# Two ordering dependencies for the w1 groups of a gated attention and MLP kernel

**Chip and metric.** One core of one Trainium2 chip. The metric is the device time of one execution in microseconds (us). The span that the profile shows is about 1.7 us shorter than that time. PE is TensorE, POOL GpSimd, ACT ScalarE, DVE VectorE and SP SyncE. The granted clock is what the trace records of PE's clock, as a share of full speed; 0.5 is called half clock here.

## What is computed

The input x has 2048 tokens of 640 features. Branch A is linear attention with 32 heads of 20; branch B is a two-stage mixer with layernorms; a sigmoid gate mixes them. Cut to what matters here:

```python
a = linear_attention(x, wqkv) @ wo           # needs phi(k), phi(q), and k^T v per head
h = gelu(layernorm(x) @ w1)                  # token shifts by 1 and 2, then
x1 = x + shift(h) @ w2
b = x1 + gelu(layernorm(x1) @ w3) @ w4
out = g * a + (1 - g) * b
```

The kernel never forms v. It builds G = x^T phi(k) (640 x 640), in five tiles of 128 rows ("features" 0 to 4), and from G and the v weights the k^T v of each head ("KV groups").

## The kernel before

The program is a list of items (matmul groups, normalizations, loads) in several streams. At build time a greedy scheduler takes the item that could start first by a rough time model, and this fixes each engine's instruction order. At run time every engine works through its own order and waits on semaphores. An item's dependency is a pair (item, lag): the named item must already have been *issued*, and with a number, the model also waits for its end. With `None` only the order is fixed.

```python
for d, lag in it["deps"]:
    if d not in done:
        ok = False
        break
    if lag is None:
        continue
    v = done[d] + 100.0
    if v > est:
        est = v
...
key = (max(est, t_pe), 0 if it["dur"] == 0.0 else 1, -cp[n])
```

Three groups of items meet in the stretch in question:

```python
# G: features 1..4 in two parts each, over token tiles 0..10 and 11..15
for i in range(1, KD):
    IT.add("GT", ("ga", i), 2.98, lambda i=i: gt_step(i, 0, NT - 5), deps=[(("k", NT - 1), 0.0)] if i == 1 else [])
    IT.add("GT", ("g", i), 1.36, lambda i=i: gt_step(i, NT - 5, NT), deps=[(("g0", NT - 1), 0.0)])

# first layernorm: statistics of a chunk of 4 tiles, then normalize a tile (both on POOL),
# then transpose it by DMA into xnT
for u in range(NT):
    if u % 4 == 0:
        IT.add("S1", ("s1", u // 4), 0.0, lambda u=u: stats1(u // 4), deps=[(("k", u + 3), 1.8)])
    ...
    IT.add("N1", ("n1", u), 0.0, lambda u=u: normalize(1, u, st1), deps=d1)
    IT.add("T1", ("t1", u), 0.0, lambda u=u: t_xn(1, u), deps=[(("n1", u), 1.1)])

# w1: four chunks of 4 token tiles, five groups of 5 matmuls each; j == 0 needs the 4 tiles
for c in range(NCH):
    for j in range(KD):
        deps = [(("t1", u), 0.9) for u in range(4 * c, 4 * c + 4)] if j == 0 else []
        if c == 0 and j == 0:
            deps.append((LAST_EXP, None))
        IT.add("W1", ("w1", c, j), 1.08, lambda c=c, j=j: w1_group(c, j), deps)
```

In the profile, G's matmuls carry line L783 (`ps<-pk_tok,x_tok`), w1's L606 (`ps<-xnT,w_59`), the KV groups' L939 (`ps<-GT,wv`). L831 is dummy matmuls of constants, which the kernel's `warmup` issues at the start.

## Time and profile before

| | before |
|---|---|
| time, median (first three runs) | 270.7 us |
| span of the profiled run | 269.1 us |
| PE busy | 97% of the span |
| mean granted clock | 0.994 |
| PE stall on the transposed x | 2.62 us |

The page's busy line, its clock by 40 slices (tenths of full speed), the shares by engine of the chain that ended last, and the w1 group with its busy time, mean, idle before it and releaser:

```profile
PE 262.0 (97%) x1729; PEld 137.1 (51%) x1729; DVE 146.7 (55%) x242; ACT 107.8 (40%) x218; POOL 92.0 (34%) x148
...
PEclk9999999999799999999999999999999999999999
...
PE 92%; POOL 4%; DMA 1%; ACT 1%; DVE 0%; issue 0%; POOLq 0%
...
L606 PE MATMUL ps<-xnT,w_59 128*128 128x512 bf16 x100 | 25.6, 399 | 2.6 <-DMA xnT<-xn 2.6
```

PE is busy nearly all the time, so a change that leaves its work as it is must remove idle time of PE or give its matmuls a faster clock. The single slice with a 7, and the 2.6 us of idle before w1, are the only blemishes after the start. PE's timeline (start, duration, line, operands, count; idle before it in brackets) places them:

```profile
53.71 12.66 PE L783 MATMUL ps<-pk_tok,x_tok 128*128 128x512 bf16 x92
68.99 5.08 PE L606 MATMUL ps<-xnT,w_59 128*128 128x512 bf16 x15 [2.62 <-DMA xnT<-xn]
73.91 1.52 PE L783 MATMUL ps<-pk_tok,x_tok 128*128 128x512 bf16 x10
75.27 1.24 PE L606 MATMUL ps<-xnT,w_59 128*128 128x512 bf16 x5
76.34 3.15 PE L783 MATMUL ps<-pk_tok,x_tok 128*128 128x512 bf16 x22
```

PE runs out of issued G work at 66.37 us and stands until tile 3 of the normalized x has landed. There was more G work, but it stood behind w1 in PE's order (the next 10 matmuls of G began at 73.91 us). The windows view over these microseconds has PE busy in the first pair of columns and the granted clock third from the end:

```profile
66.00:69.00 3.00, 0.38 (x8) 0.24 (x6) 2.93 (x3) 0.00 (x0) 3.00 (x4) 1.00 0.63 121
...
70.00:71.00 1.00, 1.00 (x5) 0.40 (x3) 1.00 (x1) 0.60 (x1) 1.00 (x2) 0.61 2.69 146
71.00:72.00 1.00, 1.00 (x3) 0.30 (x2) 0.96 (x2) 0.00 (x0) 0.80 (x1) 0.50 0.04 4
72.00:73.00 1.00, 1.00 (x4) 0.42 (x3) 0.47 (x1) 0.60 (x1) 0.00 (x0) 0.50 0.87 182
73.00:74.00 1.00, 1.00 (x5) 0.38 (x4) 0.00 (x0) 0.00 (x0) 0.68 (x1) 0.68 0.77 140
```

So the stall was followed by 3.413 us of half clock (70.22 to 73.64 us in the trace's clock record). Why tile 3 was late is read from POOL's timeline: tile 0 was normalized at 51.03 us, then came the statistics of the last chunk, then seven more tiles in a row. Tile 3 is the third of these.

```profile
51.03 0.87 POOL L628 TENSOR_SCALAR xn<-x_tok,st_54 128x640 bf16<-128x640 bf16 x1
54.76 0.26 POOL L628 TENSOR_SCALAR st_54<-lr 128x4 f32<-128x4 f32 x1 [2.86 <-ACT lr L662]
...
61.78 10.02 POOL L628 TENSOR_SCALAR xn<-x_tok,st_54 128x640 bf16<-128x640 bf16 x7
```

The chain of waits (start, duration, what) shows the three tiles and then the DMA transpose of tile 3, which landed at 68.74 us:

```profile
61.79 4.35 POOL xn L628 x3
66.16 2.58 DMA xnT<-xn
```

### The profile page before, as it was taken

To read this page: it belongs to the slowest core of one execution; us is meant where nothing else is said; L and a number is where in the kernel's file an instruction comes from. 1 tells how busy PE (TensorE), PEld (TensorE's weight loads), DVE (VectorE), ACT (ScalarE), POOL (GpSimd) and SP (SyncE) were. 2 spreads that over 40 slices of the span, in tenths; PEclk is the share of its full clock that TensorE was granted. 3 is DMA by queue.
4 is the path that set the end of the run, shared out by engine and by line. 5 is a ranking of instruction groups with operands and counts; after the bars stand their busy time and mean duration, and the time that the engine had idled before them with its cause. 6 is when DMAs were issued, how large, how long until landed. Compare 5 with 4: busy or idle time off the path is not lost.

```text
span 269.1 us, 4338 instructions
## 1 busy us (share of the span) xinstructions
PE 262.0 (97%) x1729; PEld 137.1 (51%) x1729; DVE 146.7 (55%) x242; ACT 107.8 (40%) x218; POOL 92.0 (34%) x148
## 2 busy tenths in 40 slices
PE   7999999998799999999999999999999999999995
PEld 4555555554255555555444555554555455445553
DVE  1587877899700787999796786512212121122232
ACT  3496777642126459575762202112221412121000
POOL 4013995779762007387850103101120011021020
PEclk9999999999799999999999999999999999999999
DMA  7765979732957971533856831220000200002011
GB/s 217 224 97 146 210 154 128 229 42 49 119 103 139 394 236 26 74 65 58 77 113 126 106 73 24 51 97 0 2 0 0 100 0 0 2 0 100 0 49 49
DMA packets 50355, 24.77 MB, mean 92 GB/s; under 512 B 41756, under 2 KB 48925, under 8 KB 50336
## 3 DMA queue, kind: packets, MB, share of 16 engines
q1 hardware_dynamic: 49184, 21.23, 36.3%
q0 software_dynamic: 1152, 3.28, 5.3%
q8 instruction: 13, 0.21, 0.4%
q14 instruction: 6, 0.05, 0.1%
HBM read 12.04 MB, written 2.62 MB: 55 GB/s over the span
## 4 chain that ended last, share of the span: by engine, by line
PE 92%; POOL 4%; DMA 1%; ACT 1%; DVE 0%; issue 0%; POOLq 0%
PE ps L606 61%; PE ps L1100 21%; PE ps L783 3%; PE ps L853 2%; POOL xn L628 2%; POOL st_54 L636 2%; PE ps L831 1%; PE ps L1082 1%; PE ps L1022 1%; DMA xnT<-xn 1%; PE ps L617 1%; PE ps L939 1%; PE ps L854 1%; DVE x_tok L645 0%; POOL st_54 L628 0%
## 5 line engine op out<-in xcount | busy, mean ns | idle before, releaser
L662 ACT ACTIVATE h2T<-ps 128x512 bf16<-128x512 f32 x52 | 31.0, 596 | 83.8 <-PE ps L606 83.7
L606 PE MATMUL ps<-xnT,w_58 128*128 128x512 bf16 x260 | 60.9, 379 | 0.0
L1100 PE MATMUL ps<-w_84,h2T 128*128 128x512 bf16 (+1 forms) x416 | 58.8, 299 | 0.0
L628 POOL TENSOR_SCALAR abx<-x_tok,stg 128x640 f32<-128x640 bf16 x16 | 13.9, 874 | 107.6 <-DVE x_tok L645 71.2
L1100 PEld LDWEIGHTS ps<-w_84,h2T 128*128 128x128 bf16 x416 | 32.7, 98 | 27.8 <-issue 1.3
L645 DVE SCALAR_TENSOR_TENSOR x_tok<-ps,stg,abx 128x640 bf16<-128x640 f32 (+2 forms) x17 | 14.3, 845 | 51.7 <-PE ps L1100 51.7
L606 PEld LDWEIGHTS ps<-xnT,w_58 128*128 128x128 bf16 x260 | 24.0, 98 | 24.9 <-issue 1.0
L645 DVE SCALAR_TENSOR_TENSOR abx<-ps,stg,abx 128x640 f32<-128x640 f32 x16 | 14.1, 882 | 27.9 <-PE ps L606 24.9
L606 PE MATMUL ps<-xnT,w_59 128*128 128x512 bf16 x100 | 25.6, 399 | 2.6 <-DMA xnT<-xn 2.6
L662 ACT ACTIVATE hsT<-ps 128x512 bf16<-128x512 f32 (+1 forms) x32 | 18.8, 593 | 23.0 <-PE ps L606 22.6
L662 ACT ACTIVATE Er<-ps 128x640 bf16<-128x640 f32 x32 | 22.4, 704 | 13.7 <-PE ps L606 8.5
L661 ACT ACTIVATE junk<-x_tok 128x640 bf16<-128x640 bf16 x32 | 23.6, 736 | 2.0 <-DVE x_tok L643 1.7
L783 PE MATMUL ps<-pk_tok,x_tok 128*128 128x512 bf16 (+1 forms) x160 | 24.2, 299 | 0.0
L606 PE MATMUL ps<-M_sb,pqnT 128*128 128x512 bf16 (+1 forms) x160 | 24.1, 299 | 0.0
L606 PE MATMUL ps<-w_60,hsT 128*128 128x512 bf16 (+1 forms) x160 | 23.7, 299 | 0.0
L643 DVE SCALAR_TENSOR_TENSOR x_tok<-ps,x_tok 128x640 bf16<-128x640 f32 x16 | 13.0, 821 | 19.2 <-PE ps L606 17.6
L606 PE MATMUL ps<-wkg,xT 128*128 128x512 bf16 (+1 forms) x150 | 22.6, 299 | 0.0
L606 PEld LDWEIGHTS ps<-M_sb,pqnT 128*128 128x128 bf16 x160 | 13.1, 98 | 12.2 <-issue 0.6
L628 POOL TENSOR_SCALAR xn<-x_tok,st_54 128x640 bf16<-128x640 bf16 x16 | 17.8, 1123 | 4.3 <-DMA xnT<-xn 4.3
L606 PEld LDWEIGHTS ps<-w_60,hsT 128*128 128x128 bf16 x160 | 13.2, 98 | 12.1 <-DVE Lt L636 0.3
L628 POOL TENSOR_SCALAR xn<-x_tok,st_55 128x640 bf16<-128x640 bf16 x16 | 16.8, 1057 | 4.9 <-DMA xnT<-xn 4.5
L606 PE MATMUL ps<-wq,xT 128*128 128x512 bf16 (+1 forms) x120 | 18.3, 299 | 0.0
(74 smaller groups left out, 265.1 us busy)
## 6 DMA issues: line engine op xcount, KB each, us to landing
w_58<-in_B_w_dram SPq DMA_DIRECT2D x1, 2160.0 KB, 9.6
w_84<-in_B_w_dram SPq DMA_DIRECT2D x1, 2080.0 KB, 12.3
x_tok<-in_A_x_dram SPq DMA_DIRECT2D x3, 640.0 KB, 5.9
out_dram<-x_tok SPq DMA_DIRECT2D x3, 640.0 KB, 3.5
wq<-in_A_wqkv_dram SPq DMA_DIRECT2D x5, 160.0 KB, 4.0
wkg<-in_A_wqkv_dram SPq DMA_DIRECT2D x5, 160.0 KB, 4.2
wv<-in_A_wqkv_dram POOLq DMA_DIRECT2D x1, 800.0 KB, 6.7
wo_aug<-in_A_wo_dram POOLq DMA_DIRECT2D x5, 150.0 KB, 5.1
```

Of the source, the lines that this page charges most:

```text
L606: ins = e.matmul(out_ap, l, r, start=(i == 0), stop=(i == n - 1))
L617: ins = e.transpose(o, s_, ident[:])
L628: return engf(lambda e: e.tensor_scalar(out_ap, in_ap, s1, s2, op0, op1), rd, [out_ap], cost=cost)
L636: return engf(lambda e: e.tensor_tensor(out_ap, a, b_, op), [a, b_], [out_ap], cost=cost)
L643: return dve(lambda e: e.scalar_tensor_tensor(out_ap, in0, scalar, in1, op0, op1, accum_out=accum), rd, [out_ap, accum], cost=cost + 70.0)
L645: return dve(lambda e: e.scalar_tensor_tensor(out_ap, in0, scalar, in1, op0, op1), rd, [out_ap], cost=cost)
L661: return act(lambda e: e.activation(out_ap, in_ap, func, bias=bias, scale=scale, accum_out=accum), rd, wr, cost=cost)
L662: return act(lambda e: e.activation(out_ap, in_ap, func, bias=bias, scale=scale), rd, wr, cost=cost)
L783: ins = e.matmul(o, l, r, start=(t0 + q_ == 0), stop=(t0 + q_ == NT - 1))
L831: ins = e.matmul(ps[:, b, :], ones_c[:, 0:128], ones_c[:, 128:640], start=True, stop=True)
L853: e.matmul(ps[:, b, 0:512], l, w[:, k, 0:512], start=(k == 0), stop=(k == KD - 1))
L1100: ins = e.matmul(o, l, r, start=False, stop=(i == KFF - 1))
```

## The change

The intent is to keep PE on G, which needs nothing late, until xnT is there: w1's first group may be issued only once the first part of G feature 4 has been, and chunk 1's w1 groups only behind all of G.

```diff
             if c == 0 and j == 0:
                 deps.append((LAST_EXP, None))
+                deps.append((("ga", KD - 1), None))
+            if c == 1 and j == 0:
+                deps.append((("g", KD - 1), None))
```

## The prediction

> **What bounds the kernel now.** TensorE. The page's busy table gives PE 97% of a 269.1 us span, and the chain that ended last is 92% PE. The table of who waited for whom has one real PE stall after the start: `PE ps L606 <- DMA xnT<-xn`, 2.6 us, once. The PE timeline places it: the G matmuls (L783) end at 66.37 us, the first w1 group starts at 68.99. It waits for the transposed normalized tile 3 of x, whose DMA transpose went out at 66.16 and took 2.58 us (chain of waits). POOL had run the last chunk's statistics (55.5 to 60.9 us) before normalizing tiles 1 to 3.

> The stall costs twice. The windows view shows the granted clock at 0.5 just after it; the clock record says from 70.22 us for 3.413 us[...]. The 15 w1 matmuls that began at 68.99 took 5.08 us in the chain; the 15 at 79.33, at full clock, took 3.24. So 1.84 us is clock loss.

> **What the change does.** It adds and removes no work. Compared in issue order, the rest of G feature 3 (10 matmuls, 1.36 us) and the first part of feature 4 (22 matmuls, 2.99 us) now go before the first w1 group. Then four w1 groups of chunk 0, the rest of feature 4, the fifth w1 group, the first KV group, and only then chunk 1's w1 groups. From the zb group on, PE's order is as before.

> **Critical path.** G needs nothing late, so it fills the hole: 66.37 + 1.36 + 2.99 = 70.7 us, 2 us after tile 3 landed at 68.74. The stall (2.62) and the half clock (1.84) both go: at most 4.46 us, all of it on the path, because PE runs without another stall from 69 to 265.5 us.

> Possible new waits, each checked by adding up PE durations:
> - Chunk 1's first w1 group at about 78.5 us needs tile 7, whose transpose is issued at 72.04, so lands near 74.7: slack near 4 us.
> - The KV group at about 77.5 us needs ACT's copy of the last G tile (0.70 us after about 76.6): no slack to speak of, perhaps 0.2 us lost.
> - w3's first group (114.93 us) has 1.5 us slack to the second layernorm's transposes; that chain hangs on w2 tiles 0 to 3, which move with PE, so the slack should stay.

> [...] I expect 4.3 us of gain.

> **Prediction.** 270.7 - 4.3 = 266.4 us (-1.6%), range 265.7 to 268.0. Faster by over 2% (below 265.3) 4%, within 2% 95%, slower 1%. More would need more than the whole stall and throttle.

> **What would show it.** PE's wait on `xnT<-xn` disappears; the granted clock stays 1.0 past the start (mean 1.000); first w1 matmul near 70.7 us; first KV matmul near 77.5 (85.01 before); first w3 matmul near 110.6 (114.93); PE busy falls by about 1.8 us, the span by about 4.3.

> **What would make it wrong.** A new PE stall before KV (GT copy queued behind gelus on ACT); a second-layernorm transpose chain that does not move with PE and returns the gain at w3; a new stall long enough to halve the clock again.

The sum: 2.62 + 1.84 = 4.46 us, less about 0.2 for the KV group, is the 4.3. But that the half clock came from the stall rests in the prediction only on its coming just after; e3, e5 and e6 below were made to test it.

## The result

| | before | after |
|---|---|---|
| median, first runs | 270.78 us | 266.89 us |
| ratio | | 0.9858 (0.9839 to 0.9877) |
| ratio, later repeat in five rounds | | 0.9884 (0.9861 to 0.9907) |
| span of the profiled run | 269.08 us | 265.20 us |
| mean granted clock | 0.994 | 1.000 |

A ratio is the mean time of one kernel's runs over the mean of the other's runs of the same rounds, so it is not quite the ratio of the medians. Executions over 1.5% slower than the fastest of the same kernel are left out of the means. Among the four runs before was one of 392.89 us, the first one: the ratio leaves it out, the median of 270.78 us counts it. Both ratios are within 2%.

The same lines of the page after:

```profile
PE 260.8 (98%) x1729; PEld 137.3 (52%) x1729; DVE 146.3 (55%) x242; ACT 107.9 (41%) x218; POOL 91.8 (35%) x148
...
PEclk9999999999999999999999999999999999999999
...
PE 98%; DVE 0%; POOL 0%; issue 0%; POOLq 0%
...
L606 PE MATMUL ps<-xnT,w_59 128*128 128x512 bf16 x100 | 23.9, 379 | 0.0
```

The 7 is gone from the clock row, w1 has no idle before it, and the chain no longer runs through POOL and the DMA. PE's timeline after:

```profile
54.42 17.01 PE L783 MATMUL ps<-pk_tok,x_tok 128*128 128x512 bf16 x124
71.26 4.48 PE L606 MATMUL ps<-xnT,w_59 128*128 128x512 bf16 x20
75.58 1.52 PE L783 MATMUL ps<-pk_tok,x_tok 128*128 128x512 bf16 x10
76.94 1.24 PE L606 MATMUL ps<-xnT,w_59 128*128 128x512 bf16 x5
78.02 1.21 PE L939 MATMUL ps<-GT,wv 128*128 128x120 bf16 x20
```

G now runs through in one block of 124 matmuls, and w1 and KV follow without a gap. Over the stretch where before stood and ran at half clock, the windows view after reads:

```profile
66.00:69.00 3.00, 3.00 (x28) 1.85 (x26) 2.90 (x4) 0.53 (x1) 1.75 (x2) 1.00 0.49 87
69.00:72.00 3.00, 3.00 (x24) 1.70 (x23) 2.93 (x3) 1.46 (x2) 3.00 (x4) 1.00 0.55 105
72.00:75.00 3.00, 3.00 (x16) 1.35 (x15) 0.61 (x1) 1.50 (x3) 2.56 (x3) 1.00 0.63 121
```

But the block starts 0.71 us *later* than before (54.42 against 53.71 us), in a part of the program that the change does not touch. The difference comes within the first microseconds. PE's timeline at the start, first before, then after:

```profile
4.92 0.82 PE L831 MATMUL ps<-ones_c 128*128 128x512 bf16 x2
5.58 0.72 PE L617 MATMUL ps<-ident,x_tok 128*128 128x128 bf16 x10
6.14 0.59 PE L831 MATMUL ps<-ones_c 128*128 128x512 bf16 x2
```

```profile
4.96 1.06 PE L831 MATMUL ps<-ones_c 128*128 128x512 bf16 x2
5.81 1.20 PE L617 MATMUL ps<-ident,x_tok 128*128 128x128 bf16 x10
6.85 0.59 PE L831 MATMUL ps<-ones_c 128*128 128x512 bf16 x2
```

The same ten transposes take 0.72 us before and 1.20 after. The clock records give the reason: their first record of full clock begins at 5.37 us in the profile before and at 6.79 in the profile after. I call this moment r. The trace has no record before it, so the clock row and the mean clock count the start as full; that it ran at half clock is read from the transposes, which took 0.72 us in the profile before, where they came after r, and 1.20 in the profile after, where nearly all of them came before it. The 1.42 us of difference in r, at half clock, are the 0.71 us.

From r on, the clock records of these two traces change only at whole multiples of 3.413 us. Before: full clock for 64.85 us (19.0 times 3.413), then half clock for 3.413. After: full clock for 259.41 us (76.0 times), past the end of the span. A stretch of 3.413 us, counted from r, is called a window below; it is a name for this reading of the records and no more.

So two numbers describe a profile: its r, and the time from the first matmul of the G block to the end of the span, in which r plays no part. I call the second the *rest*. Before: 269.08 - 53.71 = 215.37 us. After: 265.20 - 54.42 = 210.78. The change gained 4.59 us in the rest of this pair, and 0.71 of it was lost at the start: 3.88 us of span.

### The profile page after: what moved, and what is told of

Its sections match the earlier page's. It is cut to its first block, busy times and chain, and to the rows that moved or that the text cites. A ratio compares the mean times of both kernels' runs of the same rounds, so it can differ in the third digit from the quotient of the medians.

```text
span 265.2 us, 4339 instructions
## 1 busy us (share of the span) xinstructions
PE 260.8 (98%) x1729; PEld 137.3 (52%) x1729; DVE 146.3 (55%) x242; ACT 107.9 (41%) x218; POOL 91.8 (35%) x148
## 3 DMA queue, kind: packets, MB, share of 16 engines
HBM read 12.04 MB, written 2.62 MB: 55 GB/s over the span
## 4 chain that ended last, share of the span: by engine, by line
PE 98%; DVE 0%; POOL 0%; issue 0%; POOLq 0%
PE ps L606 61%; PE ps L1100 21%; PE ps L783 8%; PE ps L853 2%; PE ps L831 1%; PE ps L1082 1%; PE ps L1022 1%; PE ps L617 1%; PE ps L939 1%; PE ps L854 1%; DVE x_tok L645 0%; POOL ones_c L665 0%; POOLq L1226 0%
## 5 line engine op out<-in xcount | busy, mean ns | idle before, releaser
L606 PE MATMUL ps<-xnT,w_58 128*128 128x512 bf16 x260 | 60.9, 379 | 0.0
L606 PEld LDWEIGHTS ps<-xnT,w_58 128*128 128x128 bf16 x260 | 24.1, 98 | 24.8 <-issue 1.0
L606 PE MATMUL ps<-M_sb,pqnT 128*128 128x512 bf16 (+1 forms) x160 | 24.1, 299 | 0.0
L606 PE MATMUL ps<-xnT,w_59 128*128 128x512 bf16 x100 | 23.9, 379 | 0.0
L783 PE MATMUL ps<-pk_tok,x_tok 128*128 128x512 bf16 (+1 forms) x160 | 23.9, 299 | 0.0
L606 PE MATMUL ps<-w_60,hsT 128*128 128x512 bf16 (+1 forms) x160 | 23.7, 299 | 0.0
L606 PE MATMUL ps<-wkg,xT 128*128 128x512 bf16 (+1 forms) x150 | 22.6, 299 | 0.0
L606 PEld LDWEIGHTS ps<-w_60,hsT 128*128 128x128 bf16 x160 | 13.3, 98 | 12.1
L606 PEld LDWEIGHTS ps<-M_sb,pqnT 128*128 128x128 bf16 x160 | 13.2, 98 | 12.1 <-issue 0.6
L628 POOL TENSOR_SCALAR xn<-x_tok,st_54 128x640 bf16<-128x640 bf16 x16 | 17.5, 1097 | 4.5 <-DMA xnT<-xn 4.4
L606 PE MATMUL ps<-wq,xT 128*128 128x512 bf16 (+1 forms) x120 | 18.3, 299 | 0.0
L628 POOL TENSOR_SCALAR xn<-x_tok,st_55 128x640 bf16<-128x640 bf16 x16 | 16.2, 1024 | 5.0 <-DMA xnT<-xn 4.6
L628 DVE TENSOR_SCALAR Er<-Er 128x640 bf16<-128x640 bf16 x32 | 12.0, 375 | 10.3 <-ACT Er L662 10.2
(74 smaller groups left out, 266.9 us busy)
```

The costliest lines, as they stand in the source:

```text
L606: ins = e.matmul(out_ap, l, r, start=(i == 0), stop=(i == n - 1))
L628: return engf(lambda e: e.tensor_scalar(out_ap, in_ap, s1, s2, op0, op1), rd, [out_ap], cost=cost)
L783: ins = e.matmul(o, l, r, start=(t0 + q_ == 0), stop=(t0 + q_ == NT - 1))
```

## Experiments

Three questions were open. Did the gain come from the filled hole, or does the order of G, w1 and KV matter in itself? Is the half clock a consequence of the hole, and always? Is r a property of the kernel or of the execution?

| run | median us | ratio to before | r | idle of PE before w1 | half clock after the start | rest |
|---|---|---|---|---|---|---|
| before (first profile) | 270.7 | | 5.37 | 2.62 | 70.22 to 73.64 | 215.37 |
| after | 266.89 | 0.9858 | 6.79 | none | none | 210.78 |
| e1_first_only | 266.89 | 0.9860 | 7.00 | none | none | 211.11 |
| e2_second_only | 268.50 | 0.9925 | 4.68 | 1.86 | none | 212.81 |
| e3_fill | 269.74 | 0.9966 | 5.55 | 0.46 | none | 214.11 |
| e4_norm_first | 266.87 | 0.9858 | 6.86 | none | none | 210.93 |
| b1_before_again | 269.47 (1 run) | | 5.92 | 2.61 | none | 213.67 |
| b2_before_again | 269.55 (1 run) | | 5.87 | 2.62 | none | 213.68 |
| b3_before_again | 270.47 (1 run) | | 7.82 | 2.65 | none | 213.71 |
| a1_after_again | 266.95 | 0.9884 | 7.03 | none | none | 210.79 |
| e5_long_hole | 275.70 | 1.0186 | 7.27 | 5.49 | 68.71 to 75.54 | 219.38 |
| e6_long_hole_filled | 272.34 | 1.0071 | 4.70 | none | none | 216.55 |

All runs gave the correct result. The runs e1 to e4, b1 to b3 and a1 were made on one chip, e5 and e6 on another. The columns from r on are of the profiled run. "None" for the idle time means that w1 follows the matmul before it without a gap.

### One dependency without the other

Against the changed kernel, e1:

```diff
-            if c == 1 and j == 0:
-                deps.append((("g", KD - 1), None))
```

> Only the first new dependency (first w1 group after the first part of G feature 4 is issued); chunk 1's w1 groups may again go before the rest of G. Theory (the gain is the filled hole plus the half clock that followed it, and nothing else): 266.9 us within 0.7, no PE wait on xnT<-xn, no half clock after the start. Rival (getting G and the KV groups done early, the second dependency, brings part of the gain): 268 us or more, with PE waits later on.

and e2:

```diff
-                deps.append((("ga", KD - 1), None))
```

> Only the second new dependency. By issue order it alone pulls the rest of G feature 3 (10 matmuls, 1.36 us) before the first w1 group. Theory: the stall on xnT<-xn shrinks from 2.62 to about 1.26 us. If so short an idle stretch no longer triggers the half clock: 270.7 - 1.36 - 1.84 = 267.5 us; if it still does: 269.3 us. Rival (the order of KV and w2 behind G is what gained): about 266.9 us although the stall is still seen.

e1 has the same median as the changed kernel, 266.89 us, with no stall and no half clock: the first dependency is the change, as far as timed runs can tell. Its one profile has a rest 0.33 us longer than after's; five rounds would not separate that, and I have not placed it, so what the second dependency adds is at most some tenths.

e2 is the case that stands between. Its single dependency pulls only the rest of feature 3 ahead, and PE still stands. The idle stretch was expected to be 1.26 us and was 1.86, because tile 3 landed later after POOL had finished it: the issue of tile 2's transpose held SP's DMA queue for 1.87 us here and for 1.20 in the profile before, and tile 3's went out 0.47 us behind it. Why that issue took longer is open. Its rest is 0.87 us shorter than that of before without a half clock (213.68 - 212.81), near the 0.76 by which its idle stretch is shorter than the 2.62 of b2. (One of e2's other runs has a mean clock of 0.999; one window of half clock, as in the profile before, makes it 0.994.) The time of 268.5 us thus lies between the two that were expected, and excludes the rival (266.9 with the stall still seen).

### The same hole closed from the other side

e4, against the kernel before: only the order on POOL is changed, so that the tiles of chunk 0 are normalized before the last statistics. PE's order is untouched.

```diff
-IT.add("S1", ("s1", u // 4), 0.0, ..., deps=[(("k", u + 3), 1.8)])
+IT.add("S1", ("s1", u // 4), 0.0, ..., deps=[(("k", u + 3), 1.8)] + ([(("n1", 3), None)] if u == 12 else []))
```

> The kernel before with PE's order untouched, but POOL normalizes tiles 1 to 4 before it does the last chunk's statistics, so that tile 3 lands near 60 us instead of 68.74 us and the first w1 group need not wait at 66.37 us. Theory (the late tile was the whole cause): the same time as the changed kernel, 266.2 to 266.9 us, no PE wait on xnT<-xn, no half clock. Rival (issue order of G and w1 itself matters): stays above 268 us though the wait is gone.

266.87 us, with the ratio of the changed kernel to four digits. Two lines of PE's timeline in e4:

```profile
54.46 12.68 PE L783 MATMUL ps<-pk_tok,x_tok 128*128 128x512 bf16 x90
66.98 3.40 PE L606 MATMUL ps<-xnT,w 128*128 128x512 bf16 x15
```

w1 comes after the same part of G as before (some matmul records are missing, so 90 stands for 92), but without a stall. The order of G and w1 on PE therefore has no worth of its own that these runs could show (rests of 210.93 and 210.79 us). It is one of two ways to avoid the same wait.

### The half clock

e3 puts dummy matmuls of constants into the hole of the kernel before:

```diff
 def w1_group(c, j):
     cols = slice(512 * c, 512 * (c + 1))
+    if c == 0 and j == 0:
+        warmup(12, 0.0)
```

> The kernel before, with 12 matmuls of constants (2.6 us of full-clock PE work that nobody reads) just ahead of the first w1 group, so that PE is busy in the hole but no useful work moves. Theory (the half clock is the consequence of PE's idle stretch and costs 1.84 us on its own): 270.7 - 1.84 = 268.9 us, granted clock 1.0 from 10 us on, w1's first 15 matmuls take 3.24 instead of 5.08 us. Rival (the half clock comes from something else, or costs nothing on the path): 270.7 us.

It gained 0.7 us by its medians instead of 1.8, and the interval of its ratio, 0.9930 to 1.0003, does not exclude that it gained nothing. Tile 3 landed late here too, in the same way (1.85 us), so that 0.46 us of idle remained behind the filler. And the comparison failed as a test: before was about to show that it often escapes the half clock without any filler. Four runs settled that, three of them the kernel before unchanged, the fourth the changed kernel in five rounds:

> The kernel before, unchanged, one more profile. In the six profiles so far the half clock at the start ended at r = 4.68 to 7.00 us, always a whole number of 3.413 us windows before the next change of the clock. Theory: r is a matter of chance, each us of r costs 0.5 us, and the half clock in the middle comes only when nearly all of the stall falls in one window. Worked out from the profile before (r 5.37: 2.18 of the 2.62 us idle in one window, half clock) and the second-dependency run (1.86 us idle in one window, none): r up to about 5.4 to 6.0 gives the half clock and a span of 269.1 + (r - 5.37)/2; r above that splits the stall, none, and a span near 267.2 + (r - 5.37)/2. Rival: r is fixed by the kernel (5.37 again, 269.1 again), and so is the half clock.

> The same as b1_before_again, another draw of r. Theory: another r than in b1, and span and half clock follow the rule written there. Rival: the same r and span as b1.

> The same as b1_before_again, a third draw of r: the theory's span follows the rule written there for its own r, the rival's is 269.1 us again.

> The changed kernel again, timed in five rounds. Theory: its span follows 265.2 + (r - 6.79)/2 for its own r, no half clock after the start, and its runs spread by up to about 1.7 us with r; against before the ratio is 0.984 to 0.988, with before spreading more widely because its half clock comes in some runs only. Rival (r fixed by the kernel): all its runs within 0.3 us of 266.9.

The rival falls: r is 5.92, 5.87 and 7.82 us in three profiles of one and the same kernel, and none of the three has the half clock in the middle, though each has the stall in full. PE's timeline of b1:

```profile
54.06 12.66 PE L783 MATMUL ps<-pk_tok,x_tok 128*128 128x512 bf16 x90
69.33 3.40 PE L606 MATMUL ps<-xnT,w 128*128 128x512 bf16 x15 [2.61 <-DMA xnT<-xn]
```

The 15 w1 matmuls take 3.40 us here and 5.08 in the profile before. The expectation had left open what happens at r between 5.4 and 6.0, where b1 and b2 fell. Its rule without the half clock gives spans of 267.5, 267.5 and 268.4; measured 267.73, 267.65 and 268.70. The ratio of a1, 0.9884, came out just above the 0.984 to 0.988 expected. The rests of the three agree within 0.04 us, and before's first profile lies 1.69 us above them: that is the price of one half clock, half of 3.413 us. Each execution carries its mean clock as well: of the 25 runs of before in the three timed sets, 9 have a mean clock of 0.994 or 0.992, the others 1.0 (3 of 7, 1 of 11 and 5 of 7 in the sets, so the share is itself loose). Their mean span is 269.26 us; that of the other 16 is 268.05. The ten runs of the changed kernel in two sets have mean clock 1.0 and a mean span of 265.12 us. A run with the half clock thus stands 4.1 us above the changed kernel, one without 2.9 us. These means mix values of r and two chips, so their difference of 1.2 us is not the price of the half clock.

That the hole causes it, and a filler prevents it, needed a hole so long that chance plays no part: of the 5.49 us that it came to, at least 2.7 lie in one window wherever a boundary falls, more than the 2.18 above (the "about 2 us" of the expectation is read from the 1.97 and the 2.18). e5 holds back more of G, against the kernel before:

```diff
-    IT.add("GT", ("ga", i), ..., deps=[(("k", NT - 1), 0.0)] if i == 1 else [])
+    IT.add("GT", ("ga", i), ..., deps=[(("k", NT - 1), 0.0)] if i == 1 else [(("w1", 0, 0), None)] if i == 3 else [])
```

> The kernel before with the hole made longer on purpose: the first part of G feature 3 (22 matmuls, 2.99 us) may only go after the first w1 group, so PE stands from about 63.5 to 69 us or later. Counted from the first G matmul of the block to the end (so that the start's half clock drops out), before took 213.7 us without and 215.4 us with the half clock in the middle. Theory (a half clock follows whenever one 3.413 us window is idle for more than about 2 us, which a hole of 5.6 us makes certain): 213.7 + 3.0 + 0.9 to 2.3 = 217.6 to 219 us on that count, the half clock in every run (mean clock below 1.0 in each), time 273 to 275.5 us. Rival (the half clock in the profile before was an accident that has nothing to do with the hole): 216.7 us, mean clock 1.0 in most runs.

and e6 adds to that edit, as in e3, `warmup(26, 0.0)` ahead of the first w1 group:

> The same long hole, filled with 26 matmuls of constants (5.6 us at full clock), all else as in e5_long_hole. This is the test that e3_fill could not be, since before often escapes the half clock. Theory: no half clock in any run, about 216.7 us from the first G matmul to the end (up to 0.5 more if tile 3 lands late as in e3_fill), 0.9 to 2.3 us less than e5_long_hole. Rival: the same time as e5_long_hole, half clock or not.

The windows view of e5, then of e6:

```profile
64.00:67.00 3.00, 0.30 (x6) 0.12 (x3) 2.93 (x3) 1.99 (x2) 3.00 (x3) 1.00 0.34 64
67.00:70.00 3.00, 0.21 (x1) 0.14 (x2) 2.93 (x3) 0.00 (x0) 3.00 (x4) 0.79 0.63 121
70.00:73.00 3.00, 3.00 (x8) 1.06 (x7) 2.93 (x3) 0.60 (x1) 2.71 (x2) 0.50 1.09 84
73.00:76.00 3.00, 2.78 (x8) 1.11 (x8) 0.38 (x1) 0.00 (x0) 1.70 (x2) 0.58 0.61 119
```

```profile
64.00:67.00 3.00, 2.95 (x14) 1.37 (x14) 2.93 (x3) 1.33 (x2) 3.00 (x3) 1.00 0.57 109
67.00:70.00 3.00, 3.00 (x15) 1.30 (x14) 2.93 (x3) 0.00 (x0) 3.00 (x3) 1.00 0.57 109
70.00:73.00 3.00, 3.00 (x24) 1.69 (x22) 2.36 (x2) 0.60 (x1) 1.72 (x2) 1.00 1.18 115
```

All four runs of e5 have a mean clock of 0.986 or 0.987, all four of e6 one of 1.000. The rest of e6 is 216.55 us (216.7 expected). That of e5 is 219.38, a little above the range, as is its time (275.70 against at most 275.5; the verdict on its ratio, 1.0136 to 1.0237, is unclear at 2%). The half clock lasted two windows (68.71 to 75.54). In the first of them PE stood for the first 1.08 us (68.71 to 69.79), in the second it waited for nothing; before, PE worked through the whole window of half clock (70.22 to 73.64), and there was only one. Why there were two here was not shown. (The 2.78 of the last line is 0.22 short where a matmul record is missing.) PE worked at half clock from 69.79 to 75.54, which costs 5.75 / 2 = 2.9 us; e5 and e6 differ by 2.83 us in the rest, where 0.9 to 2.3 had been expected for a single window (estimate). The rival is out: in the four runs of each, this hole brought the half clock, and dummy work in it kept it away.

## Why the prediction was right, and where it was not

- **Right: PE bounds the kernel, and the stall on `xnT<-xn` was on the path.** It is gone after, and e4 shows that removing this one wait another way gives the same time. Seen over the rest, the stall was worth 213.68 - 210.79 = 2.89 us, where the prediction had 2.62. Of the 0.27 us, 0.16 is the overlap of one matmul group's modelled end with the next one's start (71.26 + 0.16 is where the 17.01 us block "ends"), which an idle time read off the profile leaves out; 0.11 I have not placed.
- **Right in mechanism, wrong in how often: "The stall costs twice."** The half clock does follow from the hole (e5, e6). But the prediction read one profile and booked 1.84 us as sure. It comes in 9 of the 25 runs before, so its mean worth over those runs is about 9/25 x 1.69 = 0.6 us, an estimate. And its size was read too high: 5.08 us came from the chain of waits. Start to start, the 15 matmuls took 73.91 - 68.99 = 4.92 us, against 3.24 at full clock, so 1.68.
- **Missing: the start.** Nothing in the prediction allowed for r. It moved the profile after by +0.71 us against the profile before, and can move one run against another by up to an estimated 1.6 us ((7.82 - 4.68) / 2 over the profiles seen), as much as half of the 3.0 us that the whole change gained in the repeat. Six runs of the changed kernel spread from 265.95 to 267.59 us, which fits, though only one of them has a trace that shows its r.
- **The sum.** The forecast gain of 4.3 us was 3.9 by the medians of the first runs and 3.0 in the later repeat (269.99 to 266.95). The time of 266.89 us lies in the range of 265.7 to 268.0 all the same: terms a little too small and too large offset each other. The time needed no luck with r: at half of each difference in r, the r seen (4.68 to 7.82) would give an estimated 265.9 to 267.4 us. The gain did need luck: the profile before, from which it was worked out, had the half clock, and in the repeat, where 1 of 11 runs before had it, the gain was 3.0.
- **Right: no new wait took the gain back.** KV's group was expected near 77.5 us with no slack; it began at 78.18 in the chain (77.47 without the late start), directly behind w1. The first w3 matmul came at 111.06 us, 3.87 earlier than before, or 4.58 with the start taken out: the whole gain of the rest arrived there and was kept to the end.
- **Off: PE busy.** It fell by 1.2 us (262.0 to 260.8), not by 1.8, since the longer half clock at the start put about 0.7 us back (the ten transposes alone took 0.48 us longer).

The clock records show what the prediction left out. r lay between 4.68 and 7.82 us over twelve profiles, and between 5.37 and 7.82 over the four of the kernel before; the changes after it came at multiples of 3.413 us from r (19.0 and 20.0 of them before, 6.83 us of half clock in e5). So the windows lay over the stall differently from one execution to the next (the boundary next to it at 66.81 us before, at 67.36 in b1). The prediction took the half clock of one profile as sure: a half clock seen once is one draw.

What stays open: whether the amount of idle time in a window decides, and with what limit, the three long runs with the half clock, why e5 had two windows of it, why one transpose took SP longer in e2 and e3, the 0.11 us, and what the second dependency adds.

## What to carry to other kernels

On an engine that is busy 97% of the time, look for the one stall that the waits name, and ask what ready work stands behind it in program order; where there is none, ask why the awaited piece is late, since both repairs were worth the same here. An idle stretch of TensorE can also be charged with the half clock behind it, but, in this case, only with its odds (1.69 us in the profile before, in 9 of 25 runs): put the multiples of 3.413 us from r, as this case's clock records have them, over the stall, and look at the mean clock of many runs before booking it. Where a few tenths of a per cent matter (r alone was worth up to an estimated 1.6 us here), compare profiles from the first instruction that the change touches, not from the start of the span.
